# A front with its own PSUM pool, a mirrored last row, V in both row groups and the residual table on GpSimd

## The chip, the core and the metric

The kernel runs on one core of a Trainium2 chip. The metric is the time of one execution on the device, in microseconds (us). Five engines work beside each other: TensorE (PE, matrix products into PSUM; its weight loads are listed as PEld), VectorE (DVE), ScalarE (ACT), GpSimd (POOL) and SyncE (SP, which here only issues DMAs). POOL, SP and ACT issue the DMAs. Each engine works through its own instructions in the order in which they were put down, and waits for others on semaphores.

## The reference

```
def reference(x, U, V, w_ch1, w_ch2):         # x: 8 x 3136 x 256, float32
    X = real(fft(fft(x, axis=1), axis=2))     # of each of the 8 batches
    h = X.transpose(0, 2, 1) @ U @ V          # U: 3136 x 32, V: 32 x 3136
    u = X + h.transpose(0, 2, 1)
    return u + relu(u @ w_ch1) @ w_ch2        # w_ch1: 256 x 1024, w_ch2: 1024 x 256
```

## The kernel before

**The whole.** A sequence of 3136 is written as 49 by 64 (N1, N2). The transform over the sequence is done in two stages of matrix products with tables of sines, which the kernel makes itself from iotas: `mask_bits` (L430, DVE) keeps the fraction of an angle, and `sin_of` (L434) takes the sine on ACT. The low rank product with U and V is put into the same tables: T (128 rows by 25 by 128) holds the second stage's table in rows 0 to 63, and V in rows 64 to 95 and, once more with the mirrored half negated, in rows 96 to 127. The transform over 256 columns is folded into the weights (`w1_fold`, L635: PE multiplies w_ch1 by the table Q, and ACT moves it to W1p). The part u that is added to the output comes from the tables Bp and Bm ("residual tables", L443).

Batches go in four pairs. Then the MLP runs in chunks of 512 columns: `mlp1` (L373) makes hT, `mlp2` (L385) the output, 128 tokens at a time. The loop at L762 puts out mlp1 of a chunk, mlp2 of the chunk before, and between them steps of the coming pair by a list of places (`plan`, L722). This is one order written out by hand (`manual_schedule`, L458): nothing is moved afterwards. The MLP from L762 on is the same code before and after, apart from its place in PSUM.

**The front**, L458 to L666, does the first batch of pair 0 alone, with the tables. It is where the change lies:

- `load_single(0)` (L108) loads x of batch 0 into X with POOL's DMAs: `rows(33, ...)` for odd rows, then x32, then `rows(31, -1, ...)` and `rows(15, -1, ...)` with the 64 lines reversed, and last the two rows of the 49th line, the second of them reversed too (L126).
- POOL makes the iotas (L465, L467, L479), issues the loads of V, w_ch1 and w_ch2 (L515 to L520), makes the angles an2 and jq (L567 to L579), and casts V into T (L584, L586).
- DVE makes the angles of ua and Fs, masks ta2, an2 and jq, and makes the residual tables' angles (L443 to L454).
- PE: 8 idle products (`keep_warm`), ups, 6 idle products, 49 products uups for the table us (L600, L604), and then the first stage of batch 0. That is `quarter_products` (L207), where four groups of 32 PSUM rows each take another 32 columns d, and `half_products` (L229), where two groups of 64 rows do. A quarter step of 8 takes 64 products for 32 columns, a half step of 8 takes 64 products for 16. `quarter_out` moves a quarter step to g in eight casts of 32x400, `half_out` a half step in two casts of 63 rows. `line32` (L194) does line 32, with the table F32, and `row32` (L204) copies it to row 63 of g with a DMA of SP.
- After these: w1_fold(0), `te_single` (L294, U's product with g), 16 products of the second stage over 64 rows and 16 with te over 128 rows (L649 to L654, to q), w1_fold(1), and then mlp1.

PSUM has three pools of two buffers for the front and the rest: psh (double banks), pso and psd. The front's products take turns in them: uups in pso in four groups, the first stage in psh, psd and pso.

What a step writes out is best seen in the two evacuations of the first stage:

```
def quarter_out(g, ps, i0, n, evac):
    for q in range(4):
        for c in range(2):
            evac(g[32 * c:32 * c + r]..., ps[32 * q:32 * q + r, 0:n, :, c, 0:NK1]...)

def half_out(g, ps, i0, n, evac):
    for h in range(2):
        evac(g[0:63]..., ps[64 * h:64 * h + 63]...)
```

Of the kernel before, what the change touches and what calls it, by code (L numbers as in the profile page):

```python
# [22 lines left out]
def kernel(  # L23
# [29 lines left out]
    psh = ctx.enter_context(tc.tile_pool(name="psh", bufs=2, space=bass.MemoryType.PSUM))  # L53
    pso = ctx.enter_context(tc.tile_pool(name="pso", bufs=2, space=bass.MemoryType.PSUM))
    psd = ctx.enter_context(tc.tile_pool(name="psd", bufs=2, space=bass.MemoryType.PSUM))

# [51 lines left out]
    def load_single(b):  # L108

        X = zpool.tile([P, 32, D], BF16, tag="z", name="X")  # L110
        nc.gpsimd.memset(X[0:PR, 31, :].bitcast(FP32), 0.0)
        yield X
        r0, L = b * N1, N1 - 1

        def rows(line, step, o):
            src = bass.AP(x.tensor, x.offset + (r0 * N2 + line) * D, [[N2 * D, L], [step * D, o.shape[1]], [1, D]])
            nc.gpsimd.dma_start(out=o, in_=src)

        rows(33, 1, X[1:2 * L:2, 0:31, :])
        yield  # L120
        nc.gpsimd.memset(x32[b][:].bitcast(FP32), 0.0)
        nc.gpsimd.dma_start(out=x32[b][0:PR:2], in_=x_pn[r0:r0 + N1, 32, :])
        rows(31, -1, X[0:2 * L:2, 0:16, :])
        rows(15, -1, X[0:2 * L:2, 16:32, :])
        nc.gpsimd.dma_start(out=X[PR - 1:PR, 0:31, :], in_=x_pn[r0 + L:r0 + N1, 33:64, :])
        nc.gpsimd.dma_start(out=X[PR - 2:PR - 1, 31::-1, :], in_=x_pn[r0 + L:r0 + N1, 0:32, :])  # L126

# [66 lines left out]
    def line32(b):  # L194
        ps = psd.tile([P, 2, D], FP32, tag="ps", name="ps32")
        o, y = ps[0:32, 0], x32[b]
        for i, (oc, t, yc) in enumerate([(o[:, 0:129], 0, y[:, 0:129]), (o[:, 1:128], 0, y[:, 255:128:-1]),
                                         (o[:, 129:256], 1, y[:, 1:128]), (o[:, 129:256], 2, y[:, 255:128:-1])]):
            nc.tensor.matmul(oc, F32[:, t], yc, start=(i == 0), stop=True, skip_group_check=True)
        z32 = cpool.tile([32, D], BF16, name=f"z32_{b}")  # L200
        nc.scalar.copy(z32[:], o)
        return z32
# [26 lines left out]
    def half_products(X, ps, i0, n):  # L229

        for i in range(n):
            for m in range(2):
                for h in range(2):
                    d = 64 * h + i0 + i
                    for c in range(2):
                        o = ps[64 * h + 32 * c:64 * h + 32 * c + 32, i]
                        nc.tensor.matmul(o[:, :, 0:NK1], X[0:PR, :, 256 - d if m else d],
                                         Fs[:, 0:3:2, c, 0:NK1] if m else Fs[:, 0:2, c, 0:NK1],
                                         start=(i % 8 == 0 and m == 0), stop=True, skip_group_check=True)

    def half_out(g, ps, i0, n, evac):
        for h in range(2):
            d0 = 64 * h + i0
            evac(g[0:63].rearrange("p k (s d) -> p s k d", s=2)[:, :, :, d0:d0 + n],
                 ps[64 * h:64 * h + 63].rearrange("p i s k -> p s k i")[:, :, 0:NK1, :])
# [191 lines left out]
    def ts(o, i, a, b, op0=AL.mult, op1=AL.add):  # L437
        if b is None:
            nc.vector.tensor_scalar(o, i, a, None, op0=op0)
        else:  # L440
            nc.vector.tensor_scalar(o, i, a, b, op0=op0, op1=op1)

    def residual_tables():  # L443
        pq = cpool.tile([P, 4], FP32, name="pq")
        qa = ypool.tile([P, 2, P], FP32, tag="y", name="qa")
        for blk in range(2):
            o = pq[:, blk:blk + 1]
            ts(sg[:, blk:blk + 1], pf[:], 64.5 - blk, None, AL.is_ge)
            nc.vector.scalar_tensor_tensor(o, sg[:, blk:blk + 1], -64.0, pf[:], op0=AL.mult, op1=AL.add)
            ts(o, o, 2.0 / D, blk / D)  # L450
            ts(pq[:, 2 + blk:3 + blk], sg[:, blk:blk + 1], 0.25, 128.25)
            ts(qa[:, blk], jf[:, 0:P], o, pq[:, 2 + blk:3 + blk])
        ts(sg[:], sg[:], -2.0, 1.0)
        mask_bits(qa[:], 16)  # L454
        return lambda: sin_of(Bp[:], qa[:], 16)
# [14 lines left out]
    nc.sync.dma_start(out=U_f, in_=moe_U.rearrange("(k2 k1) r -> k2 (k1 r)", k1=N1))  # L470
    trow = tmp([1, NK1, 64], "trow", BF16)
# [3 lines left out]
    nc.sync.dma_start(out=T[63:64, :, 0:64], in_=trow[:])  # L475
    for _ in loads:
        pass
    kio = UZ[0:64].rearrange("p a b -> p (a b)").bitcast(I32)[:, 0:64 * NK1].rearrange("p (k j) -> p k j", j=64)
    nc.gpsimd.iota(kio, pattern=[[1, NK1], [N1, 64]], base=0, channel_multiplier=0)  # L479

# [3 lines left out]
    def keep_warm(n):  # L484
        ps = pso.tile([P, 2, 2, P], FP32, tag="o", name="warm")
        for i in range(n):
            nc.tensor.matmul(ps[:].rearrange("p a s d -> p (a s d)"), idle[:, 0:P], idle[:, P:640], start=True, stop=True)
# [21 lines left out]

    pn = tmp([64, 2], "pn")  # L510
# [4 lines left out]
    nc.gpsimd.dma_start(out=uv[64:96], in_=moe_V)  # L515
    w1_f = tmp([P, 2, H], "w1_f", FP32R)
# [7 lines left out]
    ups = psh.tile([P, 2, 512], FP32, tag="h", name="ups")  # L524
# [40 lines left out]
    sin_of(Fs[:], ans[:], 16)  # L565

# [6 lines left out]
    pl = tmp([P, 1], "pl")  # L573
    tg(pl[:], pf[:], 1.0 / D, None)
    jq = ypool.tile([P, 2, P], FP32, tag="y", name="jq")
    tg(jq[:, 0, 0:65], jf[:, 0:130:2], pl[:], 128.25)
    tg(jq[:, 0, 65:P], jf[:, 2:P:2], pl[:], 128.5)
    tg(jq[:, 1, 0:64], jf[:, 1:P:2], pl[:], 128.25)
    tg(jq[:, 1, 64:P], jf[:, 1:P:2], pl[:], 128.5)  # L579
# [3 lines left out]
    for lo, hi in [(0, 9), (9, 17), (17, NK1)]:  # L583
        nc.gpsimd.tensor_copy(T[64:96, lo:hi, 0:64], Vk[64:96, lo:hi, :])  # L584
        l = max(lo, 1)
        nc.gpsimd.tensor_copy(T[64:96, l:hi, 64:128], Vk[64:96, N1 - l:N1 - hi:-1, :])  # L586
# [4 lines left out]
    mask_bits(an2[:], 16)  # L591
    mask_bits(jq[:], 16)
    bp_sin = residual_tables()

    usv = us[:].rearrange("p k (r s) -> p k s r", s=2)
    for n, (k0, k1) in enumerate([(0, 7), (7, 13), (13, 19), (19, 25)]):
        ps = pso.tile([P, 8, 2, R], FP32, tag="o", name="uups")
        for k in range(k0, k1):
            o = ps[0:64, k - k0].rearrange("p s r -> p (s r)")
            nc.tensor.matmul(o, ua[:, k], ub[:, k].unsqueeze(1).to_broadcast([64, 2, R]),  # L600
                             start=(k == k0), stop=True, skip_group_check=True)
# [4 lines left out]
        copy_act(usv[:, k0:k1], ps[0:64, 0:k1 - k0])  # L606

    g0 = gpool.tile([P, NK1, D], BF16, tag="g0", name="g")
    first.g[0] = g0
    ps = psh.tile([P, 8, 2, 2, 32], FP32, tag="h", name="tps")  # L610
    quarter_products(X0, ps, 0, 8)
    quarter_out(g0, ps, 0, 8, copy_act)
    sin_of(F32[:], an2[:], 16)
    ps = psh.tile([P, 16, 2, 32], FP32, tag="h", name="tps")
    half_products(X0, ps, 8, 16)
    half_out(g0, ps, 8, 16, copy_dve)
    Q = tmp([P, 3, P], "Q", FP32R)
    for i0, evac in [(24, copy_act), (40, copy_dve), (48, copy_dve), (56, copy_act)]:
        if i0 < 48:
            ps = psd.tile([P, 8, 2, 32], FP32, tag="ps", name="tps")  # L620
        else:
            ps = pso.tile([P, 8, 2, 32], FP32, tag="o", name="tps")
        half_products(X0, ps, i0, 8)
        half_out(g0, ps, i0, 8, evac)
        if i0 == 24:
            row32(g0, line32(0))
            sin_of(T[0:63, :, 0:64], ta2[0:63], 18)
            sin_of(Q[:, 0:2], jq[:], 16)
            nc.scalar.mul(Q[:, 2], Q[:, 1], -1.0)
        if i0 == 40:  # L630
            nc.vector.tensor_copy(T[96:128, 0:9, 0:64], T[64:96, 0:9, 0:64])
            ts(T[96:128, 1:9, 64:128], T[64:96, 1:9, 64:128], -1.0, None)
    nc.vector.tensor_copy(T[0:64, :, 64:128], T[0:64, :, 63::-1])

    def w1_fold(c, evac):  # L635
        ps = psh.tile([P, 2, 512], FP32, tag="h", name="w1ps")
# [6 lines left out]
    w1_fold(0, copy_act)  # L643
    te_single(first, 0, lambda g, te: None, psh.tile([P, 2, 512], FP32, tag="h", name="teps"))
# [3 lines left out]
    pss = [psd.tile([P, 2, 256], FP32, tag="ps", name="ps") for i in range(2)]  # L648
    pss += [pso.tile([P, 2, 256], FP32, tag="o", name="ps") for i in range(2)]  # L649
# [5 lines left out]
    w1_fold(1, copy_act)  # L655
    bp_sin()
    spread([(nc.vector, 8, 16)])(g0, tes[0])
    nc.gpsimd.tensor_copy(T[96:128, 9:NK1, 0:64], T[64:96, 9:NK1, 0:64])
    nc.gpsimd.tensor_scalar(T[96:128, 9:NK1, 64:128], T[64:96, 9:NK1, 64:128], -1.0, None, op0=AL.mult)
# [5 lines left out]
    spread([(nc.gpsimd, 16, NK1)])(g0, tes[0])  # L665
    front.__exit__(None, None, None)  # L666

    qpool[1] = ctx.enter_context(tc.tile_pool(name="qpool1", bufs=1))
# [140 lines left out]
```

## Time and profile before

| what | us |
|---|---|
| median of 6 runs | 472.77 |
| lowest, highest | 469.91, 475.04 |
| the profiled execution's own time | 472.98 |
| its span, first to last instruction | 471.2 |
| first product of X on PE (L219) | 14.43 |
| first product of w1_fold (L639) | 29.14 |
| first product of the MLP (L381) | 39.08 |

The profile is of one execution. Its page gives the busy time of each engine, the span in 40 slices of 11.8 us with a digit for each (tenths busy; PEclk is the clock that PE was granted), the DMA queues, the chain of work that ended last, and the costliest groups of instructions. A timeline lists instructions in order: start, length, engine, line, operation, tiles, count, and in brackets how long the engine sat idle before it and what released it. "issue" as releaser means that the engine waited for nothing that the profile shows. A matmul's end is modelled, so the distance between starts says more than the length of one.

### The profile page before, as it was taken

How to read it: one execution, taken by the hardware profiler on the slowest of the kernel's cores; microseconds unless marked ns; L12 is line 12 of the kernel's file. 1: busy time of each engine (PE TensorE's matmuls, PEld its weight loads, DVE VectorE, ACT ScalarE, POOL GpSimd, SP SyncE). 2: the span in 40 equal slices, each digit the busy share in tenths (PEclk: the TensorE clock that was granted, in tenths of full speed). 3: DMA queues.
4: the chain of work that ended last, by engine and by line, in shares of the span. 5: the costliest groups of instructions: out<-in, count | busy, mean ns of one | idle time of the engine just before them, and what ended most of it. 6: DMA issues, size and time to landing. Idle time of an engine off the chain costs nothing.

```text
span 471.2 us, 10923 instructions
## 1 busy us (share of the span) xinstructions
PE 441.1 (94%) x4393; PEld 316.9 (67%) x4393; DVE 229.2 (49%) x528; ACT 297.9 (63%) x431; POOL 147.6 (31%) x158
## 2 busy tenths in 40 slices
PE   5688999899989999999999999899999999999994
PEld 2575666677757776677777777677767777767763
DVE  8654288866326356646254366554244354211212
ACT  5647796677654657677655666677556655666662
POOL 8980523944160054642060045552040000000000
PEclk8558999999999999999999999999999999999999
DMA  9735265677678466586494466585593333333424
GB/s 174 212 69 74 43 182 127 182 224 178 179 147 190 96 172 148 152 256 177 110 222 108 102 170 171 149 253 155 136 157 68 68 68 68 68 68 73 95 47 90
DMA packets 58545, 63.95 MB, mean 136 GB/s; under 512 B 12868, under 2 KB 51550, under 8 KB 58366
## 3 DMA queue, kind: packets, MB, share of 16 engines
q1 hardware_dynamic: 48846, 41.42, 38.6%
q0 software_dynamic: 7248, 15.35, 14.1%
q10 hardware_dynamic: 2400, 6.49, 3.7%
q8 instruction: 34, 0.56, 0.5%
q14 instruction: 17, 0.14, 0.1%
HBM read 34.22 MB, written 32.19 MB: 141 GB/s over the span
## 4 chain that ended last, share of the span: by engine, by line
PE 70%; DVE 6%; DMA 5%; ACT 4%; issue 3%; SPq 2%; ACTq 0%; DVEq 0%
PE ops L392 29%; PE hps L381 29%; PE ops L395 4%; PE ps L323 4%; DMA out_dram<-ob 3%; ACT hT L383 2%; PE ps L180 2%; DMA g<-zturn 2%; DVE q L80 1%; SPq L407 1%; PE teps L285 1%; DVE ob L403 1%; ACT g L77 1%; PE ps L219 1%; DVE yb L131 1%
## 5 line engine op out<-in xcount | busy, mean ns | idle before, releaser
L383 ACT ACTIVATE hT<-hps 128x1024 bf16<-128x1024 f32 (+1 forms) x208 | 202.1, 975 | 123.7 <-PE hps L381 115.4
L392 PE MATMUL ops<-W,hT 128*128 128x256 bf16 x1568 | 224.8, 273 | 1.7 <-DVE W L681 1.1
L392 PEld LDWEIGHTS <-hT 128*128 128x128 bf16 x1568 | 145.1, 98 | 35.3 <-DVE ob L403 1.1
L402 DVE TENSOR_TENSOR ob<-ops,om 128x256 f32<-128x256 f32 (+1 forms) x102 | 42.2, 413 | 186.7 <-ACT om L401 169.4
L381 PE MATMUL hps<-q,W1p 128*128 128x512 bf16 (+1 forms) x448 | 104.9, 356 | 0.5 <-ACT W1p L641 0.2
L381 PE MATMUL hps<-q,W1m 128*128 128x512 bf16 x384 | 98.1, 379 | 0.5 <-ACT hT L383 0.5
L139 POOL TENSOR_TENSOR y<-xa,xb 98x1020 f32<-98x1020 f32 (+1 forms) x24 | 54.7, 2281 | 121.2 <-DMA xa<-in_x_dram 104.6
L80 DVE CAST q<-ps 128x512 bf16<-128x512 f32 (+2 forms) x120 | 64.4, 559 | 35.4 <-PE ps L323 31.0
L381 PEld LDWEIGHTS <-W1p 128*128 128x128 bf16 x448 | 40.2, 98 | 27.2 <-issue 1.7
L381 PEld LDWEIGHTS <-W1m 128*128 128x128 bf16 x384 | 35.4, 98 | 26.5 <-issue 1.4
L395 PEld LDWEIGHTS <-q 128*128 128x128 bf16 x392 | 38.4, 98 | 22.1 <-issue 1.4
L401 ACT COPY om<-ops 128x256 f32<-128x256 f32 (+1 forms) x102 | 37.0, 364 | 9.3 <-PE ops L392 8.9
L403 DVE TENSOR_TENSOR ob<-ops,om 128x256 f32<-128x256 f32 (+1 forms) x102 | 41.2, 404 | 0.0
L323 PE MATMUL ps<-T,g 128*128 128x128 bf16 (+3 forms) x400 | 37.8, 221 | 3.0 <-DMA g<-zturn 2.3
L307 POOL COPY g<-te 64x1024 int32<-64x1024 int32 (+1 forms) x22 | 23.7, 1119 | 53.3 <-DVE te L271 53.3
L395 PE MATMUL ops<-Bp,q 128*128 128x128 f16 x200 | 38.4, 219 | 0.0
L395 PE MATMUL ops<-Bm,q 128*128 128x128 f16 x192 | 36.9, 219 | 0.0
L77 ACT CAST z<-ps 128x512 bf16<-128x512 f32 x48 | 28.2, 587 | 13.0 <-PE ps L180 12.8
L323 PEld LDWEIGHTS <-g 128*128 128x128 bf16 (+1 forms) x400 | 30.0, 99 | 8.1 <-issue 3.4
L130 DVE TENSOR_TENSOR yb<-y 98x508 bf16<-98x508 f32 (+1 forms) x24 | 30.8, 1283 | 0.0
L103 POOL DMA_INDIRECT xb<-in_x_dram,idx x24 | 25.1, 1045 | 5.5 <-issue 4.6
L180 PE MATMUL ps<-yb,F 98*128 98x258 bf16 (+1 forms) x108 | 18.9, 265 | 5.1 <-DVE q L80 5.1
(135 smaller groups left out, 244.2 us busy)
## 6 DMA issues: line engine op xcount, KB each, us to landing
out_dram<-ob SPq DMA_DIRECT2D x389, 64.0 KB
xa<-in_x_dram SPq DMA_DIRECT2D x24, 392.0 KB
g<-zturn SPq DMA_DIRECT2D x6, 800.0 KB
zturn<-z ACTq DMA_DIRECT2D x9, 512.0 KB
w_f<-in_moe_w_ch_dram POOLq DMA_DIRECT2D x2, 1024.0 KB, 9.3
X<-in_x_dram POOLq DMA_DIRECT2D x4, 384.0 KB
X<-in_x_dram POOLq DMA_DIRECT2D x2, 744.0 KB, 6.9
zturn<-z ACTq DMA_DIRECT2D x3, 448.0 KB
```

What stands on the lines that cost most here:

```text
L77: nc.scalar.copy(o, i)
L80: nc.vector.tensor_copy(o, i)
L130: nc.vector.tensor_tensor(o[:, :, 1:128], i[:, :, 1:128], i[:, :, 255:128:-1], op=AL.add)
L139: nc.gpsimd.tensor_tensor(ck.y[:, 0:n, 1:256], ck.xa[:, 0:n, 1:256], rb[:, :, 255:0:-1], op=AL.add)
L323: nc.tensor.matmul(o, lt, r, start=st, stop=True, skip_group_check=True)
L381: nc.tensor.matmul(ps[:, i, 0:n], (W1p if ch.sg > 0 else W1m)[:, blk, j], q[:, blk, c0:c0 + n], start=(blk == 0), stop=(blk == 1))
L383: nc.scalar.activation(ch.h[:, 2 * jp:2 * jp + 2, 0:n], ps[:, :, 0:n], AF.Relu)
L392: nc.tensor.matmul(ps, ch.h[:, j, t * P:(t + 1) * P], W2[:, j, :], start=(j == 0 and (t % 2 == 0 or last)), stop=(j == JT - 1), skip_group ...
L395: nc.tensor.matmul(ps[:, j], q[:, j, tk], (Bp if ch.sg > 0 else Bm)[:, j], start=False, stop=False, skip_group_check=True)
L401: nc.scalar.copy(om[:, 0:n], ch.po[:, 0:n, 1])
L402: nc.vector.tensor_tensor(ob[:, 0:n, 0:P], ch.po[:, 0:n, 0], om[:, 0:n], op=AL.add)
L403: nc.vector.tensor_tensor(ob[:, 0:n, P:D], ch.po[:, 0:n, 0], om[:, 0:n], op=AL.subtract)
```

## The change

- The front gets a PSUM pool of its own, fps, with four buffers of two banks; psh, pso and psd are made after the front. All the front's products go round in fps.
- uups is done in two groups of 16 and 9 instead of four, and after it come 16 idle products of 128 columns.
- The first stage is done in three quarter steps of 8 (columns to 24) and two half steps of 8 that share one buffer, instead of one quarter step and 48 columns in half steps. DVE moves the first and third quarter step, ACT the second and both half steps. line32 stands between the two half steps.
- Batch 0's reversed last row: a third DMA of POOL loads it forward into one row of the tile q, and SP copies it from there to X, reversed. For batch 1 it is loaded as before, but earlier. The other 49th row is loaded before the two reversed blocks.
- V is loaded twice, to rows 64 to 95 and 96 to 127, and cast on 64 rows at once; the mirrored half is multiplied by +1 or -1 (vs). The copies from rows 64 to rows 96 go.
- jq is made earlier on POOL, ahead of kio; Q's sine comes right after Fs's on ACT. The residual tables' angles are made on POOL, between two parts of V; their mask stays on DVE, after T's copy. an2's mask comes after the first quarter step's casts.

```diff
@@ load_single
         rows(33, 1, X[1:2 * L:2, 0:31, :])
-        yield
+        if b == 0:
+            first.q = qpool[0].tile([P, 2, 6272], BF16, tag="q", name="q")
+            xl = first.q[0:1].rearrange("p a j -> p (a j)")[:, 0:32 * D].rearrange("p (l d) -> p l d", d=D)
+            nc.gpsimd.dma_start(out=xl, in_=x_pn[r0 + L:r0 + N1, 0:32, :])
+            yield
+            nc.sync.dma_start(out=X[PR - 2:PR - 1, 31::-1, :], in_=xl)
+            yield
+        else:
+            nc.gpsimd.dma_start(out=X[PR - 2:PR - 1, 31::-1, :], in_=x_pn[r0 + L:r0 + N1, 0:32, :])
+            yield
         nc.gpsimd.memset(x32[b][:].bitcast(FP32), 0.0)
         nc.gpsimd.dma_start(out=x32[b][0:PR:2], in_=x_pn[r0:r0 + N1, 32, :])
+        nc.gpsimd.dma_start(out=X[PR - 1:PR, 0:31, :], in_=x_pn[r0 + L:r0 + N1, 33:64, :])
         rows(31, -1, X[0:2 * L:2, 0:16, :])
         rows(15, -1, X[0:2 * L:2, 16:32, :])
-        nc.gpsimd.dma_start(out=X[PR - 1:PR, 0:31, :], in_=x_pn[r0 + L:r0 + N1, 33:64, :])
-        nc.gpsimd.dma_start(out=X[PR - 2:PR - 1, 31::-1, :], in_=x_pn[r0 + L:r0 + N1, 0:32, :])
@@ residual_tables(eng), eng = nc.gpsimd
-            nc.vector.scalar_tensor_tensor(o, sg[:, blk:blk + 1], -64.0, pf[:], op0=AL.mult, op1=AL.add)
+            eng.tensor_scalar(o, sg[:, blk:blk + 1], -64.0, pf[:], op0=AL.mult, op1=AL.add)
...
-        mask_bits(qa[:], 16)
-        return lambda: sin_of(Bp[:], qa[:], 16)
+        return lambda: mask_bits(qa[:], 16), lambda: sin_of(Bp[:], qa[:], 16)
@@ front
+    fps = tc.tile_pool(name="fps", bufs=4, space=bass.MemoryType.PSUM)
+    fpool = fps.__enter__()
+
+    def bank2(shape, name):
+        return fpool.tile([P, *shape], FP32, tag="f", name=name)
...
     nc.gpsimd.dma_start(out=uv[64:96], in_=moe_V)
+    nc.gpsimd.dma_start(out=uv[96:128], in_=moe_V)
...
     sin_of(Fs[:], ans[:], 16)
+    mask_bits(jq[:], 16)
+    Q = tmp([P, 3, P], "Q", FP32R)
+    sin_of(Q[:, 0:2], jq[:], 16)
+    nc.scalar.mul(Q[:, 2], Q[:, 1], -1.0)
...
-    for lo, hi in [(0, 9), (9, 17), (17, NK1)]:
-        nc.gpsimd.tensor_copy(T[64:96, lo:hi, 0:64], Vk[64:96, lo:hi, :])
+    def v_rows(lo, hi):
+        nc.gpsimd.tensor_copy(T[64:128, lo:hi, 0:64], Vk[64:128, lo:hi, :])
         l = max(lo, 1)
-        nc.gpsimd.tensor_copy(T[64:96, l:hi, 64:128], Vk[64:96, N1 - l:N1 - hi:-1, :])
+        tg(T[64:128, l:hi, 64:128], Vk[64:128, N1 - l:N1 - hi:-1, :], vs[64:128], None)
+
+    v_rows(0, 9)
+    bp_mask, bp_sin = residual_tables(nc.gpsimd)
+    v_rows(9, NK1)
...
-    for n, (k0, k1) in enumerate([(0, 7), (7, 13), (13, 19), (19, 25)]):
-        ps = pso.tile([P, 8, 2, R], FP32, tag="o", name="uups")
+    for k0, k1 in [(0, 16), (16, NK1)]:
+        ps = bank2([16, 2, R], "uups")
...
+    sin_of(T[0:63, :, 0:64], ta2[0:63], 18)
+    keep_warm(16, P)
...
-    quarter_products(X0, ps, 0, 8)
-    quarter_out(g0, ps, 0, 8, copy_act)
...
+    for r, evac in enumerate([copy_dve, copy_act, copy_dve]):
+        ps = bank2([8, 2, 2, 32], "tps")
+        quarter_products(X0, ps, 8 * r, 8)
+        quarter_out(g0, ps, 8 * r, 8, evac)
+        if r == 0:
+            mask_bits(an2[:], 16)
+        if r == 1:
+            sin_of(F32[:], an2[:], 16)
+    ps = bank2([16, 2, 32], "tps")
+    half_products(X0, ps, 24, 8, 0)
+    row32(g0, line32(0, bank2([2, D], "ps32")))
+    half_products(X0, ps, 56, 8, 8)
+    half_out(g0, ps, 24, 8, copy_act, 0)
+    half_out(g0, ps, 56, 8, copy_act, 8)
     nc.vector.tensor_copy(T[0:64, :, 64:128], T[0:64, :, 63::-1])
+    bp_mask()
...
+    fps.__exit__(None, None, None)
     front.__exit__(None, None, None)
 
+    psh = ctx.enter_context(tc.tile_pool(name="psh", bufs=2, space=bass.MemoryType.PSUM))
+    pso = ctx.enter_context(tc.tile_pool(name="pso", bufs=2, space=bass.MemoryType.PSUM))
+    psd = ctx.enter_context(tc.tile_pool(name="psd", bufs=2, space=bass.MemoryType.PSUM))
```

## The prediction

> **What bounds the kernel now.** I read the page first, then the timelines of TensorE (PE) and VectorE (DVE) over the first 46 us, the waits of PE there, and the windows of the front.
>
> ```profile
> PE 441.1 (94%) x4393; PEld 316.9 (67%) x4393; DVE 229.2 (49%) x528; ACT 297.9 (63%) x431; POOL 147.6 (31%) x158
> ...
> PE   5688999899989999999999999899999999999994
> ...
> PEclk8558999999999999999999999999999999999999
> ...
> q8 instruction: 34, 0.56, 0.5%
> ```
>
> PE is full from the fifth slice on. Only the first four slices of 11.8 us are loose (5, 6, 8, 8 tenths), with the clock at half in two of them. The change touches only these, so the question is how many us earlier the MLP (L381, first matmul at 39.08) starts; all after it is one PE queue and moves along.
>
> ```profile
> 14.43 1.53 PE L219 MATMUL tps<-Fs,X 98*32 98x50 f16 x61 [0.54 <-POOL pv L508]
> ...
> 15.81 1.81 PE L237 MATMUL tps<-Fs,X 98*32 98x50 f16 x92
> 20.88 1.78 PE L237 MATMUL tps<-Fs,X 98*32 98x50 f16 x93 [3.26 <-issue]
> ...
> 23.94 3.14 PE L237 MATMUL tps<-Fs,X 98*32 98x50 f16 x152 [0.90 <-ACT g L77]
> 28.25 0.97 PE L237 MATMUL tps<-Fs,X 98*32 98x50 f16 x40 [1.17 <-issue]
> 29.14 2.08 PE L639 MATMUL w1ps<-w_f,Q 128*128 128x512 f32 x4
> 31.15 2.89 PE L299 MATMUL teps<-g,us 64*32 64x129 bf16 x50
> ```
>
> The products of X take 14.43 to 29.14, though 448 matmuls need about 9 us at 20 ns. Twice PE stops inside a run of independent matmuls, for 3.26 and 1.17 us, with the releaser "issue": no engine held it. The instruction queue q8 explains it. It has 34 packets of 16 KB, 256 instructions each, and its first ones start at 18.27, 22.0, 25.6 and 29.6. PE stops at its 446th and resumes one packet after 18.27; it stops again 512 instructions on. In the program's order, block edges then lie near instructions 189, 445, 701 and 957, and each crossing asks for the block after next. From the crossing of 189 (15.05) to the restart are 5.83 us, while 2 MB of weights move; from 701 (24.4) to 28.25, with the DMA engines idle, 3.83 us. So PE is bound here by the fetch of its own code.
>
> ```profile
> 29.20:31.20 2.00, 2.00 (x7) 1.16 (x8) 0.00 (x0) 0.97 (x2) 1.25 (x4) 0.50 0.51 64
> 31.20:34.00 2.80, 2.80 (x52) 2.60 (x52) 0.00 (x0) 1.02 (x1) 2.80 (x5) 0.50 0.81 142
> 34.00:37.20 3.20, 3.20 (x33) 3.00 (x33) 1.13 (x4) 0.72 (x3) 1.78 (x4) 0.50 1.06 172
> ```
>
> Columns: length, PE, weight loads, DVE, ACT, POOL, granted clock, DMA. PE is busy all the time and still has half the clock. By the trace's clock records it becomes full at 39.15.
>
> **The change part by part.**
>
> *Start.* POOL now issues the extra load of x's last row (0.53, the row of L126) ahead of the two iotas. They end 0.5 later, so does the chain of DVE to ta; ACT's ua, which waited for rv until 9.14, starts at 9.4: +0.25. The 49 uups matmuls (54 ns each) run from 11.05 instead of 10.81; two groups in four double banks remove the 0.3 us gap at 12.2, so they end at 13.7. Then come 16 new idle matmuls of 128 columns: L487's 512 columns took 0.415, a quarter is 0.104, so 1.66. The X products start at 15.3, 0.9 late.
>
> *Last row mirrored.* The semaphores of X's loads come at 8.47 to 14.30, the mirrored row last, 0.75 after the last large block (13.55). Loaded forward as third load, it is there near 9; SP then waits for it. Behind SP's wait stands only row 32's copy, issued at 24.31, so nobody is late. POOL's semaphores for DMAs go round after eight: w1's DMA now waits for X's first load (8.47), w2's for the extra row, both long landed at 12.7, so the small POOL work behind them is not held. X is complete near 13.9, under the 15.3: worth nothing. If the idle matmuls were gone it would be worth 0.4.
>
> *Fewer products.* 24 quarter steps of 8 and 16 half steps of 8 make 320 matmuls in place of 448: 128 less at 20 ns, 2.6 us, and one block edge (957) falls out of the products. Crossing 189 comes after 13 matmuls, 15.6. The 141st matmul is reached at 18.4 (21 ns each) and waits for code. V's second load (0.39 MB) and the shift of its issue put the weights about 2.5 us later, so this request again lies among V2 and w1. I take the contended 5.83: restart at 21.4; ends 19.4 (3.83, uncontended) and 22.4 (a us more). Then 51 matmuls (1.1), 64 (1.2) and line 32 (0.5) bring 24.2, a few more the next edge, whose code comes at 21.4 + 3.83 = 25.2; the last 55 (1.05) end at 26.3. w1_fold(0) starts at 26.3 instead of 29.14: 2.8 us.
>
> The skill's page "Runtime: NRT & Kernel Launch", section "Instruction fetch mechanics", says code is fetched in 16 KiB blocks, mostly hidden by the issue rate. The blocks agree with q8; "hidden" does not, the row shows 3.26 us. By the page line 32 would run at 22.7 (ACT's r1 casts, 8 of 0.484 from 18.4, then the 0.37 of F32), w1_fold(0) at 24.7, and the next stage, bound by DVE below, at 26.8: 4.3 us instead of 2.8.
>
> *Evacuation.* DVE gets two groups of eight 32x400 casts. Nearest are its 63x400 casts, 0.576 each: 4.6 a group. Group 0 from 17.0 to 21.6, the moved mask 0.22, group 2 from 22.8 to 27.4. ACT's halves are four of 0.486, to 27.3. te_single starts after w1_fold(0), 26.3 + 2.05 = 28.4, so this is hidden by 1.0; with that cover gone, each tenth of a us per cast is 1.6 us. The cast pair runs beside POOL's work, which the 63x400 and 63x800 ones did too.
>
> *POOL.* Residual tables leave DVE, where they ran from 17.95 to 23.67 and held the first cast of g until 23.59. On POOL: nine small ones of about 0.3 and two of 128 columns near 0.5, 3.5 us. V costs copies by elements, not partitions: 1.19 and 2.25 us; the sign form lies between a cast (1.17 per 512) and L659 (2.82 per 1024), so 1.4 and 2.8. L658 and L659 (3.9) go, and DVE's two copies (0.64). POOL's X1 memset comes near 30.6, not 29.33, its loads land near 43; they are read at 55.0 before, 52 after: hidden by 9 us. The spread of te ends near 36.7 and is read near 45. T's first nine rows are there at 22, its rest at 30.4, read at 33 and 38.5.
>
> *PSUM.* The four double banks go round: each slot's last reader (ACT's us copy 14.5, DVE's group 0 at 21.6, ACT's r1 22.3, te's copies during the lines) is done before its next writer. Q moves forward onto ACT, free at 12.
>
> *Clock.* The skill's page "TensorE: Matmul & The Clock Gate", section "What's actually happening", says a busy window of about 3.4 us brings the full clock. Taken plainly, the idle matmuls would give it at once: w1_fold, te_single and the two line stages take about half (te_single 1.57 at 78.61 against 2.89), about 4 us more. The windows above speak against: fully busy, 0.50 throughout. Clock changes at 5.01, 8.43 and 39.15 fit that raster, but only dense 128x128 work filled the last window. 1.7 dense us followed by 98x32 products and a 3 us hole will not hold it. I take nothing; ends 0 and 4.
>
> *Sum.* 0.9 late, 2.6 fewer matmuls, 1.1 from the shorter second stop: 2.8 us. Span 471.2 becomes 468.4; the execution's own 472.98 becomes 470.2. The median shown, 472.77, is 0.2 lower, so 470.0.
>
> **The rivals.** *Warm clock too* (chance 0.27): the idle matmuls bring the full clock and it lasts, or code arrives in time. For: the last busy window did switch at 39.15. 2.8 + 4 to 4.3 + 4 gives 466 to 464.5; I put 465.2.
>
> *Nothing left* (0.13): the later start keeps w1 in front of both code requests; twice 5.83 gives w1_fold(0) at 28.3, and the clock, whose switch at 39.15 met the MLP's first matmul at 39.08, comes up to a window (3.4 us at half speed, 1.7) later. 0.8 gained less 1.7: 473.7. This is also the case where the change doesn't do what it says.
>
> *Slower by the casts* (0.12): DVE's casts of group 0 and 2 are stretched by POOL's strided work, now without a pause from 19 to 30.
>
> ```profile
> 18.11 1.04 DVE L449 SCALAR_TENSOR_TENSOR pq<-sg,pf 128x1 f32<-128x1 f32 x1
> 19.19 0.15 DVE L441 TENSOR_SCALAR pq<-pq 128x1 f32<-128x1 f32 x1
> ```
>
> One-column instructions took 1.04 against 0.15 while POOL's casts ran. te_single would be no earlier than 31.15 from 0.86 us a cast on (17.0 + 0.22 + 16 casts), and 1% late from 1.15. At 1.2: DVE done at 36.4, +5.3, 478. Against: 63x400 casts beside L659 took 0.576.
>
> **How the numbers follow.** Forecast 0.48, the rivals 0.27, 0.13, 0.12. 1% (4.7 us) is about what a measurement of this kernel can tell from no change. Faster by that: the warm clock, 0.27, and 0.04 of the forecast where the uncontended end meets an early clock: 0.31. Slower: 0.12 and 0.02 of the second rival, 0.14. Between: 0.55. The forecast's own range is 468.6 to 471.2 from the fetch ends (4.3 to 1.8), and 1 us on each side for the runs' spread. The range over all reaches from the warm case to the second rival: 464.5 to 474.0.
>
> **What would show it.** Right: X products from about 15.3; one stop of 2 to 4 us marked "issue" in the third group and a short one near 24 to 25; L652 at 25 to 27.5; DVE casts of 0.58; granted clock 0.50 until the MLP. Wrong: clock 1.00 in the products or in te_single at 1.6 us, no stop, or te_single waiting for DVE.

## The result and the profile after

| | before | after |
|---|---|---|
| median of the runs, us | 472.64 (71 runs) | 472.27 (34 runs) |
| lowest, highest | 469.59, 479.39 | 466.32, 478.04 |
| profiled execution's own time | 472.98 | 473.00 |
| its span | 471.2 | 471.2 |

The two medians are over all runs; of the runs that the comparison keeps, the ratio after to before is 0.9959, with a 95% interval of 0.9939 to 0.9978. That is 1.9 us less (1.0 to 2.9), about 470.7. The forecast was 470.0, and "within 1%" its likeliest case. The two profiled executions have the same span, so the gain is not to be read off their ends: it has to be followed through the trace.

The three rows of the page that were shown of before (engines, PE's busy tenths and its clock in 40 slices of 11.8 us), now after:

```profile
PE 442.1 (94%) x4281; PEld 315.4 (67%) x4281; DVE 227.9 (48%) x525; ACT 297.8 (63%) x429; POOL 150.5 (32%) x168
...
PE   6598988899998999999999999999999999999995
...
PEclk9957998999999999999999999999999999999999
```

The clock is now full in the first two slices (8, 5 before), lower in the fourth (7), and dips in the seventh (8), where it was full before. PE's digits are hardly better in the second to fourth slice (5, 9, 8 against 6, 8, 8), and in the sixth and seventh they are 8 where both were 9.

PE's timeline through the front, after:

```profile
14.58 2.36 PE L222 MATMUL tps<-Fs,X 98*32 98x50 f16 x141 [0.64 <-ACT us L73]
22.15 1.34 PE L222 MATMUL tps<-Fs,X 98*32 98x100 f16 x50 [5.21 <-issue]
...
25.89 1.26 PE L240 MATMUL tps<-Fs,X 98*32 98x50 f16 x56 [1.01 <-issue]
27.08 2.08 PE L652 MATMUL w1ps<-w_f,Q 128*128 128x512 f32 x4
...
35.28 2.06 PE L652 MATMUL w1ps<-w_f,Q 128*128 128x512 f32 x4
38.44 3.57 PE L384 MATMUL hps<-q,W1p 128*128 128x512 bf16 x8 [1.11 <-ACT W1p L654]
```

The end of the same stretch before, which the lines shown so far leave out:

```profile
37.22 2.05 PE L639 MATMUL w1ps<-w_f,Q 128*128 128x512 f32 x4
39.08 1.08 PE L381 MATMUL hps<-q,W1p 128*128 128x512 bf16 x4
40.39 1.02 PE L381 MATMUL hps<-q,W1p 128*128 128x512 bf16 x4 [0.23 <-ACT W1p L641]
```

Read the starts against before: w1_fold(0) at 27.08 instead of 29.14 (2.06 earlier), w1_fold(1) 1.94 earlier, but the MLP's first product only 0.64 earlier. 1.3 us are lost between the last two lines. A wait of 1.11 us for ACT's move of W1p is new there (before, only the second four products waited for that move, 0.23 us), and the eight hps products take 3.57 us, which is half speed (TensorE does four in 1.02 at full clock). So by the first output of the MLP (L406) the lead of 0.64 has become 0.59 us *late*.

The windows of the same stretch (columns: length, PE, weight loads, DVE, ACT, POOL, granted clock, share of DMA, GB/s):

```profile
32.00:35.20 3.20, 3.20 (x33) 2.98 (x32) 1.07 (x4) 0.67 (x3) 2.60 (x7) 0.50 0.59 87
35.38:38.80 3.42, 2.31 (x7) 1.29 (x6) 1.53 (x3) 1.75 (x3) 3.23 (x5) 0.50 0.99 177
```

PE is busy throughout the first, with the second stage's products; in the second it is busy 2.31 of 3.42 us, because of the wait. The clock stays at half in both, and for one more window. By the clock records it was full from 11.49 to 21.73 and again from 42.21; before, again from 39.15.

A second loss comes at 66 us, on three engines at once:

```profile
66.54 2.94 DVE L442 TENSOR_SCALAR F<-ang,mb 98x384 f16<-98x384 f32 x2 [1.01 <-ACT ang L437]
66.56 2.37 POOL L142 TENSOR_TENSOR y<-xa,xb 98x1020 f32<-98x1020 f32 x1 [7.22 <-ACT ang L437]
72.42 0.73 PE L222 MATMUL ps<-Fs,X 98*32 98x100 f16 x32 [2.66 <-DVE g L76]
```

The same two before:

```profile
65.95 0.75 DVE L439 TENSOR_SCALAR F<-ang,mb 98x384 f16<-98x384 f32 x2 [1.02 <-ACT ang L434]
66.91 2.35 POOL L139 TENSOR_TENSOR y<-xa,xb 98x1020 f32<-98x1020 f32 x1 [8.17 <-ACT hT L383]
```

There DVE's two instructions for the table F took 0.75 us together, and POOL's y began after them. After, y begins in the same moment, and F takes 2.94: the first of its two instructions takes 2.61, until y is done, the second its usual 0.41. The casts behind F are late, PE waits 2.66 us for them, and the clock falls to half from 72.9 to 76.3. The output is then 4.42 us later than before's. Yet the whole of it is made good: the offset is 3.3 at 150 us, 1.5 at 210, 0.3 at 319 and 0.07 at the end, as waits of before (3.6 us of PE for q's casts, 2.3 for zturn's DMA) shrink to 0.9 and 1.4.

### The profile page after: what moved, and what is told of

Read it like the earlier page. It is cut to its first block, busy times and chain, and to the rows that moved or that the text cites. A ratio compares the mean times of both kernels' runs of the same rounds, so it can differ in the third digit from the quotient of the medians.

```text
span 471.2 us, 10714 instructions
## 1 busy us (share of the span) xinstructions
PE 442.1 (94%) x4281; PEld 315.4 (67%) x4281; DVE 227.9 (48%) x525; ACT 297.8 (63%) x429; POOL 150.5 (32%) x168
## 4 chain that ended last, share of the span: by engine, by line
PE 75%; ACT 4%; DMA 4%; DVE 4%; issue 2%; SPq 1%; ACTq 0%; DVEq 0%
PE ops L395 31%; PE hps L384 31%; PE ops L398 4%; PE ps L326 4%; DMA out_dram<-ob 2%; PE ps L183 2%; ACT hT L386 2%; ACT g L73 2%; DMA g<-zturn 2%; PE teps L288 1%; SPq L410 1%; DVE ob L406 1%; PE ps L222 1%; DVE q L76 1%; DVE F L442 1%
## 5 line engine op out<-in xcount | busy, mean ns | idle before, releaser
L384 PE MATMUL hps<-q,W1p 128*128 128x512 bf16 (+1 forms) x448 | 106.4, 361 | 1.3 <-ACT W1p L654 1.1
L406 DVE TENSOR_TENSOR ob<-ops,om 128x256 f32<-128x256 f32 (+1 forms) x102 | 41.2, 404 | 0.0
L133 DVE TENSOR_TENSOR yb<-y 98x508 bf16<-98x508 f32 (+1 forms) x24 | 22.5, 938 | 0.0
```

The lines of the kernel that those rows point to most:

```text
L384: nc.tensor.matmul(ps[:, i, 0:n], (W1p if ch.sg > 0 else W1m)[:, blk, j], q[:, blk, c0:c0 + n], start=(blk == 0), stop=(blk == 1))
L406: nc.vector.tensor_tensor(ob[:, 0:n, P:D], ch.po[:, 0:n, 0], om[:, 0:n], op=AL.subtract)
```

## The experiments

All but the last are edits of the changed kernel. What sums up each: start of w1_fold(0), start of the MLP's first product, time at which the full clock came back, and how much later than before's the first and the last output are put together (L406, L403 before), each from one profiled execution; then the ratio to the kernel before, timed.

| kernel | w1_fold(0) | MLP | full clock | first output | last output | ratio, 95% interval |
|---|---|---|---|---|---|---|
| before | 29.14 | 39.08 | 39.15 | 0 | 0 | 1 |
| after | 27.08 | 38.44 | 42.21 | +0.59 | +0.07 | 0.9959, 0.9939 to 0.9978 |
| e1_shift64 | 27.12 | 38.41 | 37.04 | -1.02 | -1.00 | 0.9964, 0.9929 to 0.9999 |
| e2_wlate | 27.94 | 40.82 | 43.96 | +2.75 | +0.60 | 1.0005, 0.9976 to 1.0034 |
| e3_vonce | 27.39 | 38.74 | 37.61 | -0.69 | +0.45 | 1.0006, 0.9973 to 1.0039 |
| e4_vonce_wlate | 24.82 | 37.74 | 41.40 | -0.17 | -3.29 | 0.9982, 0.9954 to 1.0011 |
| e5_nowarm | 26.54 | 37.92 | 36.98 | -1.51 | -6.25 | 466.69 us, one run |
| e6_nomirror | 26.73 | 38.09 | 42.22 | +0.41 | +0.79 | 473.81 us, one run |
| e7_psum2 | 30.68 | 42.06 | 41.19 | +2.63 | +2.14 | 475.11 us, one run |
| e8_fold1_f | 28.01 | 35.70 | 30.46 | -3.71 | -4.77 | 0.9941, 0.9901 to 0.9981 |
| e9_nowarm_t | | | | | | 0.9989, 0.9954 to 1.0023 |
| e10_best1 | 26.58 | 34.36 | 29.19 | -5.06 | -7.09 | 0.9889, 0.9847 to 0.9930 |
| e11_best2 | 29.80 | 40.57 | 45.86 | +3.40 | +0.41 | 1.0010, 0.9973 to 1.0047 |
| e12_before_moves | 28.68 | 36.30 | 32.10 | -2.95 | -7.57 | 0.9972, 0.9930 to 1.0013 |

e9's profiled execution is the slowest of its twelve (474.24), so its trace is not used; e8's clock record begins only at 30.46. Between the first and the last output the distance to before changes by anything from 4.7 us less (e5) to 1.1 more (e3); a single trace therefore shows where a stage went, and only the timed ratio what it was worth. Each ratio is to runs of before made beside that kernel's own.

**Is the stop the fetch of code?** Theory: PE stops at fixed places of its own instruction stream, and when it goes on is set by what else DMA carries. Four kernels:

```diff
@@ e1_shift64
     ups = bank2([2, 512], "ups")
+    keep_warm(64, 32)
@@ e2_wlate: the loads of w1_f and w2_f stand after v_rows(0, 9)
-    w1_f = ...; nc.gpsimd.dma_start(out=w1_f[:], ...); g1 = ...; nc.gpsimd.dma_start(out=w2_f, ...)
...
     v_rows(0, 9)
+    w1_f = ...; nc.gpsimd.dma_start(out=w1_f[:], ...); g1 = ...; nc.gpsimd.dma_start(out=w2_f, ...)
@@ e3_vonce: rows 96 to 127 of T are copied from rows 64 to 95, as before
-    nc.gpsimd.dma_start(out=uv[96:128], in_=moe_V)
+    nc.vector.tensor_copy(T[96:128, 0:9, 0:64], T[64:96, 0:9, 0:64])
+    ts(T[96:128, 1:9, 64:128], T[64:96, 1:9, 64:128], -1.0, None)
@@ e4_vonce_wlate: both
```

> The changed kernel with 64 idle products of 32 columns added ahead of ups, where PE waits for U anyway. Theory (the fetch of PE's code): 128 instructions more stand ahead of the X products, so the block edges fall 64 products earlier. The stop of 5.2 us after the 141st X product goes; one after the 77th takes its place, short (0 to 1.5 us), since its code is asked for during uups, and a longer one (2 to 4 us) after the 205th. w1_fold(0) starts near 25.5 instead of 27.1. Rival (PE waits for some engine, PSUM or the data of X at that point): the stop stays after the 141st product with its 5 us, and w1_fold(0) at 27 or later.

> The changed kernel with the loads of w_ch1 and w_ch2 issued after T's first rows (about 20 instead of 13.7 on GpSimd). Theory (the fetch waits behind the loads of the weights): the first stop shrinks from 5.2 to 2 to 3.5 us, as V's two loads are still in its way; w1_fold(0) starts near 25 to 26, then bound by w_ch1's landing. Rival (fetch time is fixed, whatever the DMA engines do): the stop stays at 5 us.

> The changed kernel with V loaded once and copied from rows 64 to rows 96 on chip, as in the kernel before. Theory: V's second load lies ahead of the fetched code; without it the fetch packet moves from 19.6 to about 18, the stop from 5.2 to 3.5 us, w1_fold(0) from 27.1 to 25.5. VectorE's two copies (0.64) and GpSimd's (3.9) come back under cover. Rival (the second load costs nothing): stop and w1_fold(0) unchanged.

> Both: V loaded once, w_ch1 and w_ch2 issued after T's first rows. Theory: nothing is moved while the first block is asked for, so the request takes 3.8 us as it did before with the DMA engines idle: the stop shrinks to 2 us, w1_fold(0) starts near 24.5 to 25.5 and may wait for w_ch1. Time 1 to 3 us under the changed kernel's 472.3. Rival (fixed fetch time): 5 us stop, same time.

PE's timeline of e1, with 64 more idle products ahead of those of X:

```profile
15.96 1.52 PE L222 MATMUL tps<-Fs,X 98*32 98x50 f16 x77
19.42 2.51 PE L222 MATMUL tps<-Fs,X 98*32 98x100 f16 x115 [1.94 <-issue]
...
24.80 1.02 PE L240 MATMUL tps<-Fs,X 98*32 98x50 f16 x46 [2.71 <-issue]
```

The stop has moved from after the 141st product to after the 77th: 64 products inserted, 64 products earlier; a second one, 2.71 us, stands 128 products on. Nothing in the data changes there, so the place belongs to the instruction stream. (In e5 and e10 below, with 16 idle products fewer, it comes after the 157th, 16 later.) What ends it: PE goes on 2.4 to 2.7 us after a packet of the instruction queue starts, in each of the ten traces used that stop there: 18.27 and 20.88 before, 19.64 and 22.15 after, 16.82 and 19.42 here. And PE's timeline of e4, which leaves the DMA queues alone while the code is wanted:

```profile
16.15 3.45 PE L222 MATMUL tps<-Fs,X 98*32 98x50 f16 x191
...
23.20 0.28 PE L202 MATMUL ps<-x,F 98*32 98x129 bf16 x2 [2.60 <-ACT F L437]
...
28.53 2.86 PE L302 MATMUL teps<-g,us 64*32 64x129 bf16 x50 [1.66 <-DMA g<-z]
```

All 192 products of the three quarter steps run through without a stop. e3, with V loaded once, still has it (3.92 us, and its packet starts at 20.37, not earlier than the changed kernel's 19.64); e2, with the weights late, keeps 0.43. In both, the products also began later, since X itself waited for its DMA (2.31 and 3.37 us), which can take a part off the stop. So the stop is a wait for code, and it went where neither V's second load nor the weights were in the queues (e4). That these loads alone set its length is not shown: e6 below issues all four as the changed kernel does, and its packet starts at 16.90. And e4's ratio is 0.998: the time goes into line 32's table F32 (2.60), the DMA of row 32 (1.66) and the same wait for W1p (1.11). The first two lay under the stop. e2 is no faster either: besides X's wait, w1_fold(0) waits 2.01 for its late weights. My expectations for the place of the stop held; those for w1_fold(0) in e1 and e3 (25.5 against 27.12 and 27.39) and in e2 (26 at the latest, 27.94), for e3's packet (18), and for e4's time (1 to 3 us under the changed kernel's, 472.12 measured) did not.

**Which part of the change makes the front shorter?** Single parts were undone:

```diff
@@ e5_nowarm
-    keep_warm(16, P)
@@ e6_nomirror: load_single for batch 0 as before
-            nc.gpsimd.dma_start(out=xl, in_=x_pn[r0 + L:r0 + N1, 0:32, :])
-            nc.sync.dma_start(out=X[PR - 2:PR - 1, 31::-1, :], in_=xl)
+        nc.gpsimd.dma_start(out=X[PR - 2:PR - 1, 31::-1, :], in_=x_pn[r0 + L:r0 + N1, 0:32, :])
@@ e7_psum2
-    fps = tc.tile_pool(name="fps", bufs=4, ...)
+    fps = tc.tile_pool(name="fps", bufs=2, ...)
-    pss = [bank2([2, 256], "ps") for i in range(4)]
+    pss = [fpool.tile([P, 2, 256], FP32, tag="s", bufs=4, name="ps") for i in range(4)]
```

> The changed kernel without the 16 idle products of 128 columns ahead of the products of X (12.87 to 14.4 in its trace). If those 16 bring the full clock that the products of X had in the changed kernel (record 1.0 from 11.49 to 21.73), the clock stays 0.50 here until the MLP, and the first group's products take 0.020 or more us each instead of 0.016. If the clock comes from the uups products or from the idle ones at the start, it is 1.00 here as well, and X starts about 1.2 us earlier, at 13.3 to 13.9 (its own rows land at 14.1 to 14.2, so the wait is then on DMA X). The stop for code does not get shorter either way: it ends when the code lands, at 22 to 23; w1_fold(0) at 26.5 to 27.5. Time 471 to 474 either way.

> The changed kernel with the loads of x in the old order (the reversed row last, straight from HBM on GpSimd's queue, not mirrored on chip). The prediction's step says that the mirror is worth 0: rows 15 to 0 land last or within 0.5 us of the reversed row (before: 13.55, 14.0, 14.3), and X products start after the uups products and the 16 idle ones anyway. Then the X products start within 0.5 us of 14.58, w1_fold(0) within 0.5 us of 27.08, and the time is within 1.5 us of the changed kernel. The rival, that the mirror is what lets the products start at 14.58, gives X waiting for DMA X by 0.5 us or more and w1_fold(0) later by as much.

> The changed kernel with two double banks for the front's pool instead of four (the four one-bank tiles of the first line stage have banks of their own). If four double banks are what lets the products run ahead of the casts, group 2 of the products waits here for the casts of group 0 (DVE until 20.4) and the 24 to 56 group for ACT's moves of group 1; since the stop for code holds TensorE to about 22.2 anyway, the first of these waits is hidden, the second costs at most 1 us: w1_fold(0) at 27 to 28.5. If the double banks don't matter, w1_fold(0) stays within 0.3 us of 27.08. Time 471 to 475.

PE's timeline of e6:

```profile
19.62 0.96 PE L215 MATMUL tps<-Fs,X 98*32 98x100 f16 x49 [1.06 <-issue]
...
25.53 1.27 PE L233 MATMUL tps<-Fs,X 98*32 98x50 f16 x56 [2.24 <-issue]
26.73 2.08 PE L644 MATMUL w1ps<-w_f,Q 128*128 128x512 f32 x4
```

Without the mirror the products start at 15.37, later than expected because uups ran at half clock in that execution, but with no wait for DMA, and w1_fold(0) is at 26.73: in this one execution the mirror is worth nothing, as the prediction had it. The stops are otherwise divided than in the changed kernel (1.06 and 2.24 against 5.21 and 1.01), though V's two loads and the weights are issued within 0.15 us of the same times; why the code came earlier here stays open. With two double banks PE's timeline has two waits in place of the stops:

```profile
22.54 1.61 PE L222 MATMUL tps<-Fs,X 98*32 98x100 f16 x64 [3.78 <-DVE g L76]
...
29.10 0.37 PE L202 MATMUL ps<-x,F 98*32 98x129 bf16 x2 [3.80 <-DVE g L76]
```

The first lies where the stop would be; the second is whole, and w1_fold(0) comes at 30.68, 3.6 later than with four and later than before. I had put 28.5 as the latest. The four double banks carry the front: they let DVE's 16 casts of 0.58 us lie beside the products.

e5's one execution was 6.3 us ahead of before's at the last output (471 to 474 us was expected, 466.69 came). The same kernel, timed:

> The kernel of e5_nowarm (the changed kernel without the 16 idle products of 128 columns) again, now timed. e5's profile ended 6.3 us earlier than the kernel before's: 1.5 at the MLP's first output, where the changed kernel's was 0.6 later. Theory: the 16 idle products bring full clock to the products of X, which then wait for code anyway, and the window in which the clock comes back falls behind the start of the MLP; without them the time is 1 to 3 us under the changed kernel's, a ratio to before of 0.988 to 0.994. Rival: the window falls by chance in each execution, idle products or not; then the ratio is that of the changed kernel, 0.996 within 0.002, and e5's 466.7 was one lucky execution.

It has 0.9989 over twelve runs, with an interval that reaches the changed kernel's 0.996. So the rival fits and the theory doesn't: the idle products are worth nothing that can be told, and 466.69 was one lucky execution. It is still instructive. In e5 the clock was half during the products of X, and w1_fold(0) was no later for it, so the full clock that the changed kernel has there is spent waiting for code. And its MLP ran at full clock from 36.98, though its first product waited the same 1.11 us.

**Is it the switch of PSUM pools and the clock's window?** In the kernel before, the first tile of the MLP's products (hps) did not wait for the move of w1_fold(1), and the second did: in psh the two buffers take turns, and the second has w1_fold(1)'s. After, the first waits for that move, though it reads only columns 0 to 255 of W1p and w1_fold(1) writes 512 to 1023. So it isn't the data. The move is the last reader of the pool fps, which is closed before psh is made. Theory: not shared banks but the closing makes the wait. So w1_fold(1) was moved up behind w1_fold(0), which also makes one dense stretch of 8 products. The table F was made earlier, to keep it off y.

```diff
@@ e8_fold1_f
     w1_fold(0)
+    w1_fold(1)
...
-    w1_fold(1)
     bp_sin()
...
-            place([lambda: rest[0]()], 10, 11)
+            place([lambda: rest[0]()], 9, 10)
@@ e10_best1: as e8, keep_warm(16, P) left out, and
+            place([lambda: rest[0]()], 7, 8)
```

> The changed kernel with two moves: w1_fold(1) stands directly after w1_fold(0), and the table F of the second pair is made one step of the plan earlier. Theory: the first product of the MLP waits for ACT's move of w1_fold(1) only since the two PSUM pools follow one another; with the fold early that wait (1.11 us on TensorE) goes, and the MLP starts at 37.0 to 37.6 instead of 38.44. And F, made earlier, no longer lies beside GpSimd's y (L142): its two instructions take 0.75 us together instead of 2.94, TensorE's wait for the casts near 70 is under 1 us instead of 2.66, and the clock stays 1.00 there. Without later slack that is 1 + 2 us: 469; since the trace of the changed kernel had made good all of its 4 us by the end, I expect 470.5 to 472.5. Rival: the wait at the first product of the MLP has its cause in the banks themselves, and stays at 1 us or more, on another mover.

> The changed kernel without the 16 idle products, with w1_fold(1) directly after w1_fold(0), and with the table F three steps of the plan earlier (e8 had moved it by one, and it met GpSimd's y again, 2.66 us). If the moves add up: first product of the MLP at 35 to 36, full clock from a window within the two folds (30 to 34) in most executions, F in 0.75 us, and no half-clock window between 66 and 85; 464 to 468, a ratio of 0.983 to 0.991. If the later stages make good what the front loses, whatever it is, the ratio stays at e8's 0.994 or above.

PE's timeline of e10:

```profile
26.58 3.31 PE L651 MATMUL w1ps<-w_f,Q 128*128 128x512 f32 x8
29.82 1.59 PE L302 MATMUL teps<-g,us 64*32 64x129 bf16 x50
...
34.36 1.90 PE L384 MATMUL hps<-q,W1p 128*128 128x512 bf16 x8 [0.94 <-DVE q L76]
```

and its windows around the switch:

```profile
25.77:29.18 3.41, 3.41 (x46) 2.89 (x47) 3.34 (x5) 2.43 (x5) 3.33 (x2) 0.50 0.04 11
29.18:32.60 3.42, 3.42 (x73) 2.71 (x73) 1.64 (x4) 1.57 (x2) 3.04 (x4) 1.00 0.00 0
```

With w1_fold(0) at 26.58, 0.5 earlier than in the changed kernel, the MLP starts at 34.36, 4.1 earlier. The clock comes back at 29.19, inside the two folds: te_single takes 1.59 us against 2.86, eight hps 1.90 against 3.57. In e8 the MLP came sooner than the 37.0 to 37.6 expected (35.70), since the clock came back early there too, and the time was lower as well (468.26, where 470.5 to 472.5 was expected). A wait of 0.94 is left in both: in e8 down to ACT's sine for Bp, in e10 to DVE's cast of q. That is just under the bound that I had set for the rival, the banks, and it is on another mover, as the rival had it; on the pools of the kernel before the same order leaves 0.53, on ACT's cast of q (e12, below). So the wait for W1p goes when w1_fold(1) is not the last in the pool, and the kernel before, with the same order but no switch of pools, didn't have it on its first tile. Whether the closing ties the two or a bank that both pools use, no run here separates, and whether some 0.4 us of the 0.94 belong to the new pools stays open. F one step earlier met y again in e8 (2.66 us); three steps earlier (e10) it takes 0.89 and no half-clock window follows. e10 takes 465.84 us (six runs), 0.9889 of before: the fastest version found.

> e10's kernel, and the front's transfers and tables in another order: V's second copy issued after the two te memsets, w1 and w2 after the first rows of T, F32's table and T's mirrored half before the first casts, the third group's casts alternating between ScalarE and VectorE. If a transfer that leaves the code's queue alone is what the front lacks, there is no stop over 1 us in the products of X, and w1_fold(0) comes at 23.5 to 25.5; the first product of the MLP 1 to 2 us earlier than e10's, the ratio 0.002 to 0.004 lower. If other waits take the place of the stop, as in e4, the MLP starts within 0.5 us of e10's and the ratio is within 0.002 of it.

e11 moved the transfers as well (V's second copy after te's memsets, w1 and w2 after v_rows(0, 9), F32's table and T's mirrored half ahead of the casts, copy_alt for the third group). All 192 products of the quarter steps run from 14.81 without a stop; PE's timeline shows what took its place:

```profile
29.80 3.75 PE L649 MATMUL w1ps<-w_f,Q 128*128 128x512 f32 x8 [6.33 <-DMA w_f<-in_moe_w_ch_dram]
```

V's second copy lands at 20.5, v_rows(0, 9) waits for it in POOL's queue, so w1 is issued only at 24.27 and lands at 29.7. The ratio is 1.001: the 23.5 to 25.5 that was expected for w1_fold(0) is missed by more than 4 us, the two folds in a row did not bring the clock back (45.86), and the gain of e10 is lost again to one load behind one wait.

**How much of e10 is the change?** The same two moves on the kernel before:

```diff
@@ e12_before_moves, on the kernel before
     w1_fold(0, copy_act)
+    w1_fold(1, copy_act)
...
-    w1_fold(1, copy_act)
...
-            place([lambda: rest[0]()], 10, 11)
+            place([lambda: rest[0]()], 7, 8)
```

> The kernel before (not the changed one) with two of e10's moves: w1_fold(1) directly after w1_fold(0), and the table F three steps earlier. It tells how much of e10's 0.989 belongs to the change. If the change's front is worth its 2 us and the moves only let them through: the two folds start at about 29.1 here and not at 26.6, the clock comes back within them, the first product of the MLP comes at 36.5 to 37.5 (e10: 34.4; before: 39.1), and the ratio is 0.993 to 0.997. If the moves are all, the ratio is e10's, 0.987 to 0.991. If they do nothing without the change (before, the MLP did not wait for w1_fold(1)'s move), 0.998 or more.

```profile
28.68 3.68 PE L639 MATMUL w1ps<-w_f,Q 128*128 128x512 f32 x8
...
36.30 2.07 PE L381 MATMUL hps<-q,W1p 128*128 128x512 bf16 x7 [0.53 <-ACT q L77]
```

The MLP starts at 36.30 here, 1.94 after e10's, and w1_fold(0) 2.10 after. The ratio, 0.9972, is just above what was expected, and its interval reaches 1; e10's ends at 0.9930, where this one begins. So the moves alone do little that can be told, the change alone 0.4%, and both together 1.1%. In the traces the change's front gives its 2 us where the wait behind it is taken away; the two ratios are of different sets of runs, and their intervals touch.

## Why the prediction was right, and where not

*The number: right, and in part by luck.* The sum took a gain of 2.8 us at w1_fold(0) to the end. In the trace shown 2.06 of it came, 0.64 was left at the first product of the MLP, and nothing at the end; the 1.9 us of the comparison lie in other executions. That the two figures are so near each other is not the sum's merit alone.

*Products and stops: right, with one term too small.* The mechanism was the one shown by e1 and e4. From the restart after the stop to w1_fold(0) the sum had 26.3 - 21.4 = 4.9 us, and the trace 27.08 - 22.15 = 4.93 (8.26 before). The term that was off is the stop's end. The sum let 5.83 us pass from the crossing of block edge 189; it was about 7.3 (from about 14.8 to 22.15), with the code's packet at 19.64 instead of 18.27. Why it was longer is not settled: V's second load lands at 18.77, ahead of the packet, but without it (e3) the time from that crossing was still about 6.5, and with it, in e6, about 4. The sign put on record, one stop of 2 to 4 us, was passed with 5.21. So w1_fold(0) gained 2.06 instead of 2.8, within the forecast's own 1.8 to 4.3. The "Runtime: NRT & Kernel Launch" page of the Trainium skill, section "Instruction fetch mechanics", calls the crossing of a block "mostly hidden"; here it cost 5.21 and 1.01 us, and nothing in e4, where the queues were free when the code was fetched.

*Start: 0.7 late in the sum, too pessimistic.* The sum had 15.3; the products began at 14.58, since uups already ran at full clock from 11.49. It didn't matter: the products only reached the stop earlier.

*Mirror, casts, POOL.* The mirror was worth nothing (e6); DVE's casts took 4.64 us a group against 4.6, and te_single never waited for DVE; the sign form was 2.06 and 3.81 against 1.4 and 2.8, X1's memset at 31.87 against 30.6, and nobody waited for either. The slower rival is out.

*PSUM: right for the front, wrong at its end.* "Each slot's last reader is done before its next writer" held inside fps. The step that failed is the sentence under the page, "all after it is one PE queue and moves along". The sum took the gain at w1_fold(0) to the end. It left out that psh is now opened after fps is closed; the first product of the MLP then waits for fps's last reader. That wait is 1.11 us; going by the windows below, the hole also cost the window that would have brought the clock back; and the lead was gone by the first output. And it left out that a shift of the front moves DVE's F against POOL's y.

*Clock: taken as nothing, and it is half of the story.* "0.50 until the MLP" was wrong in both directions: full from 11.49 to 21.73, where it was spent on a wait for code, and half until 42.21, 3.8 us into the MLP. Full clock in the products of X was one of the signs of being wrong that stand on record.

In the 13 traces used here the clock stays at half or at full for multiples of 3.41 us, but for the ends of the record. In all of them, once w1_fold has begun, it comes back in the front at the end of a window of 3.41 us in which PE stood still for at most 0.3 us and which holds 1.7 us or more of the 512-column products (w1_fold, hps). It did not come back after a window with 2.0 us of w1_fold and the rest nearly all te_single (before, 28.9 to 32.3), nor after the next, as busy, with te_single and second-stage products, nor after one with 2.3 us of w1_fold and hps and a hole of 1.1 (after, 35.4 to 38.8). This is no rule for other products: in e11 a window full of the small products of X (15.1 to 18.6) did bring it. Where the windows fall differs from one execution to the next. "TensorE: Matmul & The Clock Gate", section "What's actually happening", states as much, a free-running window of 3413 ns; that any busy window will do is not what these traces show, and what counts as busy stays open.

Which share of the 1.9 us gained comes from executions whose window falls well can't be read from one trace. What the runs show is this: of the 71 runs of before on which the experiments' ratios rest, with a complete clock record, two had a mean clock of 0.975 or more; of 23 such runs of after, made at another time, nine, with a median of 470.0 us against about 472 for the rest. So with the change the clock is at half for less time in some executions, and the shown one, at 0.972, is not among them. The warm-clock rival has a part in the result; that it explains all of it is not shown.

## What to carry to other kernels

A gain in the front of a kernel must be followed past the first buffer that changes hands: where one PSUM pool is closed and another opened, look whether the first product after waits for the last reader before (1.11 us here), and whether the hole costs a window of the clock as well. Try dense products together rather than between small ones: with two folds in a row the clock came back at 32.10 instead of 39.15 on the kernel before (e12), and at 29.19 on the changed one (e10), though not in e11, where the load came late. When PE is about to run hundreds of small products, look what bulk loads are in flight beside the fetch of their code: with fewer of them the stops went (e4, e11). After removing a stop, look for the waits that lay under it before counting its length as gain: e4 removed 6 us of stops and gained nothing that could be measured.

## What was not expected of the hardware

Two instructions on SBUF can hold each other up for most of their length. DVE's tensor_scalar of 98x384 (fp32 to fp16, two of them 0.75 us) took 2.30 to 2.94 us in the six traces where POOL's tensor_tensor of 98x1020 (2.37) began with it or up to 0.6 us ahead. Where it began 0.4 and 0.5 us after F (e4, e2), F took its 0.75, and y 2.57 and 2.46. "SBUF — State Buffer" in the skill, section "SBUF: two separate sides", describes a shared pair of ports that is locked for a whole instruction, which fits: who comes first holds the other up. T's mirrored copy on DVE (64x1600) fits less well: begun 0.21 us after POOL's tensor_scalar of 3.81 us (28.00), it took 2.30 us against 0.61 before, but ended 1.3 us ahead of it.
